# A gated scan with a two-layer expert: the scheduler charges for same-engine results, and the weight range checks move behind the last move of x

## The chip, the cores and the metric

The kernel runs on one core of one Trainium2 chip. The metric is the device time of one execution in microseconds (us), the median of three timed runs.

## What is computed

Two stages follow each other. The first is a gated linear attention with a complex decay per channel, 4 batches by 8 heads by 768 positions with 48 channels a head. Its output, read as 3072 tokens of 384 values, goes through two matrix products with a clipped square between them. Cut to what matters:

```python
mag = np.sqrt(a_re * a_re + a_im * a_im)
scale = np.minimum(mag, 0.999) / (mag + 1e-06)
a_re_n, a_im_n = (a_re * scale, a_im * scale)
for t in range(S):
    new_re = ar * S_re - ai * S_im          # ar, ai: column t of a_re_n, a_im_n
    new_im = ar * S_im + ai * S_re
    S_re, S_im = (new_re + kv, new_im)      # kv: outer product of k[t] and v[t]
    y[:, :, t] = np.einsum('bhd,bhde->bhe', q[:, :, t], S_re)
h = x @ w_in                                # x: y as (3072, 384); w_in (384, 2048)
g = np.where(pos, h, np.where(neg, 0.0, (h + beta) ** 2 / (4.0 * beta)))
return g @ w_out                            # w_out (2048, 384)
```

## The kernel before, in words

The 3072 tokens are cut into 12 units of 256 positions, three units to a batch. Each unit is handled by `gates` and then `attend`. `gates(u)` turns the decay into prefix sums of its logarithm and of its angle (scans on DVE, logarithms, exponentials and sines on ACT), and multiplies k and q with the results. The two large products at its end (L664, in `turn`) give a cosine part, written into the tile x, and a sine part, written into kq. `spread` then moves these, in five DMAs each, into the tiles hd, which have one head side by side with its partner (L674 and on). A unit has two chunks of 128 positions. `attend(u)` forms the scores of a chunk (sc, L816), masks them (am, L824, on DVE), transposes the keys (tp, L760, copied to kT by ACT), multiplies keys with values (dp, L789), adds that to a running state st, and adds the state's and the mask's share into yp (L855, L863). ACT copies yp into xr, and a rest of it into ys.

Two units make a block, so there are six blocks, 0 to 5. When the last yp of a block is copied, six small DMAs (xr<-ys, L367) move the rest into xr. That is the hand-over of x. `split` then writes x as a rounded part xH (ACT, L948) and a remainder xL (DVE, L955), and `moe(blk)` runs 16 steps f. A step has nine matmuls into h (L978: three parts j by the products of xH and xL with the two parts of the weight), an ACT relu into s (L1003, block 0 has two more ACT instructions), DVE's maximum and product into g (L1022 and L1030), ACT's rounded copy gh (L1036) and DVE's remainder gl (L1040), and, three steps later, nine matmuls into the output sums o (L1053). h has two buffers. After the last step ACT copies o to ob (L1080), and three DMAs write it out. While PE works on one block, the other engines prepare the units of the next one, and PE takes their scores and values in between.

The weights come in as 16 packed loads of 768 KB. `weights` unpacks each with three DVE instructions (L395, L404, L413), an ACT copy for the rounded part (L419), and either one DVE subtraction (L424) or four PE matmuls with two ACT copies (L433, L434, L448) for the remainder. The first `LO_PE` of them take the PE way. `ranges(k)` loads each of the 16 packed weights a second time into a tile chk (L380, called at L453 and on) and takes two sums over it on ACT (L461 and L469) to learn whether all weights lie in the range for which the fast path is exact. The results wsum are read once, after the last matmul. chk shares four slots "g" with the tiles ai, x and kq of the units, in a fixed turn.

The order of the work is not written by hand. Each instruction is recorded in a `Plan` with its engine, a cost in ns, what it reads and writes, and, for some, a due time. `Plan.order` runs a list schedule over them: at each point it takes, on the engine that can start soonest, the ready instruction with the earliest due time. An instruction is ready when all that it depends on have ended, plus a delay `LAT` if the earlier one ran on another engine. `emit` writes the instructions in the order of their planned starts, and the engines run that order. Instructions with no due time that comes from a matmul, as the checks, are taken last. Between two PE instructions with a planned gap, `warm` puts matmuls that nobody reads (idle, L1102) until the first one of `moe` has been issued.

Where the table of constants at the top is spoken of: `SLACK` stretches the due times, `EARLY` is the share of block 0 in which the attention of block 1 is due, `HOLD` decides whether an engine leaves a ready instruction for one that is due sooner but not yet ready, and `ABS_ACT` is the number of units whose absolute value runs on ACT and not on DVE.

Of the kernel before, what the change touches and what calls it, by code (L numbers as in the profile page):

```python
# [18 lines left out]
P = 128  # L19
# [15 lines left out]
NBLK = len(BLOCKS)  # L35
# [14 lines left out]


LAT = {"PE": 260, "DVE": 190, "ACT": 190, "SP": 0, "POOL": 200}
DMA_FIX, DMA_END, DMA_ISSUE, LANES = 2400, 50, 470, 8
LOAD, MOVE = 410.0, 240.0
TABLE = 1294
FIRST = 63000
SLACK = 0.96
LAG = 3
SPREADS = 0
SPREAD = ("SP", "ACT")  # L60
HOLD = {'DVE': (0.3, 20000.0), 'ACT': (0.3, 20000.0)}
WINDOW = (0.0, 0.7)
EARLY = (0.0, 0.6)
HEAD = ((15000, 8000), (8000, 2000))
HOME = 4
SPARE = 1
LEAD = 9000
WARM = 0.75
ABS_ACT = 3
LO_PE = 5  # L70
INFLATE = 1.6
SPLIT_DUE = 3000

# [38 lines left out]
class Plan:  # L112
# [3 lines left out]
    def __init__(self):  # L116
        self.ops = []
        self.slots = {}
        self.glued = {}

    def tile(self, slot, make):
        t = Tile_(make, self.slots.get(slot))
# [32 lines left out]
    def order(self):  # L155
        ops = self.ops
# [7 lines left out]
        for i in range(n - 1, -1, -1):  # L164
            eng, cost, _, _, d, dma = ops[i]
# [26 lines left out]
        while done < n:  # L192
            if forced:
                i = forced.pop()
                e = ops[i][0]
                t = max(free[e], ready[i])
            else:
                best = None
                for e in free:
                    while avail[e] and avail[e][0][1] in taken:  # L200
                        heapq.heappop(avail[e])
                    while wait[e] and wait[e][0][1] in taken:
                        heapq.heappop(wait[e])
                    if avail[e]:
                        t = free[e]
                    elif wait[e]:
                        t = max(free[e], wait[e][0][0])
                    else:
                        continue
                    if best is None or t < best[0]:  # L210
                        best = (t, e)
                t, e = best
                while wait[e] and wait[e][0][0] <= t:
                    _, i = heapq.heappop(wait[e])
                    if i not in taken:
                        heapq.heappush(avail[e], (due[i], i))
                d, i = heapq.heappop(avail[e])
                if e in HOLD:
                    late = t + ops[i][1]
                    soon = [  # L220
                        (r, j)
                        for r, j in wait[e]
                        if j not in taken
                        and r < late
                        and due[j] + HOLD[e][1] < d
                        and late - r > HOLD[e][0] * (r - t)
                    ]
                    if soon:
                        heapq.heappush(avail[e], (d, i))
                        free[e] = min(soon)[0]  # L230
                        continue
            taken.add(i)
            eng, cost, _, _, _, dma = ops[i]
            start[i] = t
            free[e] = t + cost
            if dma:
                q = queue.setdefault(eng, [0.0] * LANES)
                t = max(t, q[-LANES])
                q.append(max(t + DMA_FIX, q[-1]) + dma)
                end[i] = q[-1] + DMA_END  # L240
                start[i] = t
                free[eng] = t + cost
            else:
                end[i] = t + cost
            done += 1
            for s in succ[i]:
                left[s] -= 1
                lat = 0 if (ops[s][0] == eng or dma) else LAT[eng]
                ready[s] = max(ready[s], end[i] + lat)
                if not left[s]:  # L250
                    enable(s)
            nxt = self.glued.get(i)
            if nxt is not None and not left[nxt]:
                forced.append(nxt)
# [46 lines left out]
def gated_scan_moe(  # L301
# [32 lines left out]
    pl = Plan()  # L334
# [44 lines left out]
    def load(k, raw):  # L379
        nc.sync.dma_start(raw.rearrange("p n t -> p (n t)"), wl[k].bitcast(U32))  # L380
# [72 lines left out]
    def ranges(k):  # L453
        RAW = tl(turn_of("g", 4), [P, 2 * DM, 2], U32, f"chk_{k}")
        top, low = (lambda: RAW.get()[:, :, 1]), (lambda: RAW.get()[:, :, 0])
        N = 2 * DM
        pl.op("SP", DMA_ISSUE, lambda: load(k, RAW.get()), w=[RAW], dma=P * N * 8 / LOAD)
        pl.op(
            "ACT",
            act(N, acc=True) + 50,  # L460
            lambda: A_.activation(  # L461
                low().bitcast(F32), top().bitcast(F32), AF.Abs, accum_out=wsum[:, 0, k : k + 1]
            ),
            w=[RAW],
        )
        pl.op(
            "ACT",
            act(N, ptr=True, acc=True) + 50,
            lambda: A_.activation(  # L469
                low().bitcast(F32),  # L470
                low().bitcast(F32),
                AF.Relu,
                bias=c_tin,
                scale=-1.0,
                accum_out=wsum[:, 1, k : k + 1],
            ),
            w=[RAW],
        )
# [5 lines left out]
    def gates(u):  # L484
# [3 lines left out]
        N = NJ * U  # L488
# [32 lines left out]
            )  # L521

        def ve(cost, fn, r, w):
            pl.op("DVE", cost, fn, r=r, w=w)

        ac(A, A, AF.Relu, [a], [a], accum_out=acc(0))
        if u > 1:
# [29 lines left out]
        )  # L557
        for j in range(NJ):
            prev = state[:, 0, j : j + 1] if part else 0.0
            ve(  # L560
                100 + U / 0.48,
                lambda j=j, prev=prev: V_.tensor_tensor_scan(  # L562
                    X0()[:, j],
                    X0()[:, j],
                    c_top.to_broadcast([P, U]),
                    prev,
                    op0=ALU.add,
                    op1=ALU.min,
                ),
                [STATE[0]] if part else [],  # L570
                [x0],
            )
        dst = fdec[:, b] if last else state[:, 0]
        ve(80, lambda: V_.tensor_copy(dst, X0()[:, :, U - 1]), [x0], [STATE[0]])
        ac(X1, X0, AF.Exp, [x0], [x1], True, scale=-1.0)
# [8 lines left out]
        ac(I, I, AF.Arctan, [], [i], True)  # L584
        for j in range(NJ):
            prev = state[:, 1, j : j + 1] if part else 0.0
            ve(
                100 + U / 0.48,
                lambda j=j, prev=prev: V_.tensor_tensor_scan(  # L589
                    A()[:, j],  # L590
# [6 lines left out]
                [i] + ([STATE[1]] if part else []),  # L597
                [a],
            )
        c = 1.0 / (2 * math.pi)  # L600
        ve(
            dve(N, True),
# [115 lines left out]

    carry = {}
    xs = {}  # L720

    def attend(u):
        b, part = divmod(u, NPART)
# [114 lines left out]
        def values(c, ams, st):  # L838
# [32 lines left out]
            def tail():  # L871
# [14 lines left out]
                if ub == nb - 1 and c == NC - 1:  # L886
                    for e in range(2):
                        for j in range(NJ):
                            p = 80 * e + 16 * j
                            dma(  # L890
                                16 * T * 4,
                                lambda j=j, e=e: XR.get()[64 * e + D : 64 * e + 64, j],
                                lambda p=p: REST.get()[p : p + 16],
                                r=[REST] + [(XR, q * CH) for q in range(T // CH)],
                                w=[(XR, (e, j))],
                            )

            r = [*ams, V, *hd] + ([st] if st else [])
            return [((16 if st else 8) * 110 + 400, run, r, YP, tail)]
# [63 lines left out]
    def moe(blk):  # L963
# [110 lines left out]
                gemm2(k - LAG)  # L1074
        for m in range(NJ):
            OB = tl(turn_of("s", 3), [P, T], F32, f"ob_{blk}_{m}")
            pl.op(
                "ACT",
                act(T, psum=True),
                lambda m=m, OB=OB: A_.copy(OB.get(), PO[m].get()),  # L1080
# [1 line left out]
                w=[OB],  # L1082
                due=t0 + STEP * (NF + LAG + 1.5),
            )
            dma(
                P * T * 4,
                lambda m=m: out[BLOCKS[blk][0] : BLOCKS[blk][-1] + 1, m].rearrange("n p t -> p n t"),
# [297 lines left out]
```

## Time and profile before

| what | us |
|---|---|
| median of three timed runs | 597.65 |
| lowest and highest of them | 594.56, 598.12 |
| the profiled execution's own time | 595.56 |
| its span in the profile | 593.8 |
| PE busy in the span | 563.2 (95%) |
| DVE busy | 448.7 (76%) |
| ACT busy | 390.3 (66%) |
| mean granted PE clock | 0.982 of full |

The span runs from the first to the last instruction of the profiled execution. Its own time is 1.76 us longer, for what lies around the span. The busy shares are means over a start in which PE waits for its first input, a long middle in which PE is the engine that never rests, and an end in which DVE and ACT have little to do.

### The profile page before, as it was taken

The page shows a single profiled execution, that of the slowest core. Times are in us where ns is not written, and L with a number is a line of the kernel's source. Part 1 is how long each engine was busy: PE and PEld are TensorE (multiplying, and loading weights), DVE is VectorE, ACT ScalarE, POOL GpSimd, SP SyncE. Part 2 cuts the span into 40 slices and gives each one's busy share as a digit, 9 for nine tenths or more (in the row PEclk, how much of TensorE's full clock was granted, in tenths as well). Part 3 has the DMA queues.
Part 4 walks back from the last instruction along what each step waited for, and adds up shares of the span by engine and source line. Part 5 has one row for each costly group of instructions (what it writes and reads, how often), then busy time and mean ns, then how long its engine had stood idle before and what let it go on. Part 6 is the DMA issues. An engine that isn't in the chain of part 4 may idle for free.

```text
span 593.8 us, 9849 instructions
## 1 busy us (share of the span) xinstructions
PE 563.2 (95%) x3874; PEld 475.9 (80%) x3874; DVE 448.7 (76%) x637; ACT 390.3 (66%) x632; POOL 1.5 (0%) x18
## 2 busy tenths in 40 slices
PE   6978988999899999999999999999999999799994
PEld 5767887888788888888888888888888887588883
DVE  3998899999989898897887977977954543555452
ACT  7757779998986767666657586556567475543332
POOL 0000000000000000000000000000000000000000
PEclk9887999999999999999999999999999999999998
DMA  8468363653540610532502512503576744010001
GB/s 350 181 194 233 114 218 110 204 223 108 180 160 19 172 70 0 160 147 67 173 2 81 174 54 81 159 2 95 187 237 167 232 146 175 14 55 0 1 0 59
DMA packets 21798, 74.25 MB, mean 125 GB/s; under 512 B 3888, under 2 KB 8496, under 8 KB 21744
## 3 DMA queue, kind: packets, MB, share of 16 engines
q1 hardware_dynamic: 21744, 73.55, 38.7%
q8 instruction: 32, 0.52, 0.4%
q14 instruction: 22, 0.18, 0.1%
HBM read 48.76 MB, written 4.72 MB: 90 GB/s over the span
## 4 chain that ended last, share of the span: by engine, by line
PE 56%; DVE 18%; DMA 11%; ACT 8%; SPq 3%; issue 2%; DVEq 0%; ACTq 0%
PE o L1053 23%; PE h L978 22%; DMA chk<-in_wl_dram 7%; PE sc L816 4%; SPq L367 3%; PE yp L863 2%; ACT ai L518 2%; PE yp L855 2%; PE dp L789 2%; DVE x L562 2%; ACT chk L469 2%; DVE g L1022 1%; DVE ai L589 1%; ACT x L518 1%; PE tp L760 1%
## 5 line engine op out<-in xcount | busy, mean ns | idle before, releaser
L978 PE MATMUL h<-xH,wi 128*128 128x512 f32 x576 | 180.5, 394 | 6.5 <-DVE g L1022 6.5
L1053 PE MATMUL o<-gh,wo 128*128 128x512 f32 x576 | 179.8, 393 | 0.2 <-ACT gh L1036 0.2
L978 PEld LDWEIGHTS h<-xH,wi 128*128 128x128 f32 x576 | 105.9, 188 | 28.9 <-DVE g L1022 8.2
L1053 PEld LDWEIGHTS o<-gh,wo 128*128 128x128 f32 x576 | 106.4, 188 | 22.3 <-ACT gh L1036 0.8
L1022 DVE TENSOR_TENSOR g<-h,s 128x512 f32<-128x512 f32 x96 | 65.9, 686 | 67.5 <-ACT s L1003 61.5
L1053 PE MATMUL o<-gl,wo 128*128 128x512 f32 x288 | 112.4, 390 | 0.0
L978 PE MATMUL h<-xL,wi 128*128 128x512 f32 x288 | 112.3, 390 | 0.0
L1036 ACT CAST gh<-g 128x512 fp32r<-128x512 f32 x96 | 59.2, 618 | 61.0 <-DVE g L1030 59.9
L1040 DVE TENSOR_TENSOR gl<-g,gh 128x512 fp32r<-128x512 f32 x96 | 66.0, 688 | 36.1 <-ACT gh L1036 35.6
L1003 ACT ACTIVATE s<-h,cst 128x512 f32<-128x512 f32 x96 | 65.7, 685 | 39.5 <-PE h L978 35.0
L518 ACT ACTIVATE ai<-ai 128x768 f32<-128x768 f32 x51 | 42.9, 843 | 33.7 <-DVE ai L609 10.9
L1053 PEld LDWEIGHTS o<-gl,wo 128*128 128x128 f32 x288 | 54.1, 188 | 12.1 <-DVE gl L1040 0.6
L978 PEld LDWEIGHTS h<-xL,wi 128*128 128x128 f32 x288 | 54.1, 188 | 11.6
L1030 DVE SCALAR_TENSOR_TENSOR g<-s,g 128x512 f32<-128x512 f32 x80 | 55.3, 691 | 2.6
L816 PE MATMUL sc<-hd 96*128 96x128 f32 x384 | 49.7, 278 | 0.0
L816 PEld LDWEIGHTS sc<-hd 96*128 96x128 f32 x384 | 46.9, 191 | 2.2
L863 PE MATMUL yp<-am,V 128*64 128x128 f32 x384 | 36.4, 279 | 1.3 <-DVE am L824 1.3
L1102 PEld LDWEIGHTS idle<-mask,ident 128*128 128x128 f32 x226 | 31.6, 221 | 2.6 <-POOL mask masks.py:66 1.7
L1102 PE MATMUL idle<-mask,ident 128*128 128x128 f32 x226 | 32.1, 305 | 1.7 <-POOL mask masks.py:66 1.7
L824 DVE TENSOR_TENSOR am<-sc,mask 128x512 f32<-128x512 f32 x48 | 32.5, 682 | 1.1 <-PE sc L816 0.9
L855 PE MATMUL yp<-hd,st 96*64 96x128 f32 x320 | 32.1, 278 | 1.0 <-DVE am L824 1.0
L461 ACT ACTIVATE chk<-chk 128x768 f32<-128x768 f32 x16 | 14.5, 905 | 21.5 <-DMA chk<-in_wl_dram 21.5
(87 smaller groups left out, 637.6 us busy)
## 6 DMA issues: line engine op xcount, KB each, us to landing
chk<-in_wl_dram SPq DMA_DIRECT2D x16, 768.0 KB, 5.2
kq<-in_kq_dram SPq DMA_DIRECT2D x12, 768.0 KB, 4.8
ai<-in_ari_dram SPq DMA_DIRECT2D x11, 768.0 KB, 6.2
hd<-x SPq DMA_DIRECT2D x24, 288.0 KB, 3.8
hd<-kq SPq DMA_DIRECT2D x24, 288.0 KB, 4.6
raw_i<-in_wl_dram SPq DMA_DIRECT2D x8, 768.0 KB, 6.0
raw_o<-in_wl_dram SPq DMA_DIRECT2D x8, 768.0 KB, 4.6
V<-in_v_dram SPq DMA_DIRECT2D x12, 384.0 KB, 3.2
```

Source lines behind the costliest of these rows:

```text
L518: lambda: A_.activation(out(), src(), f, **kw),
L816: PE_.matmul(SC.get()[:, i, :], t[:, 0, cs], t[:, 1, cs], start=True, stop=True)
L855: PE_.matmul(o, st.get().rearrange("p h e -> p (h e)")[:, lo : lo + 64], head(h)[:, 1, cs], start=True, stop=False,)
L863: PE_.matmul(o, V.get()[:, c, lo : lo + 64], ams[g].get()[:, 2 * pr + e, :], start=st is None, stop=True,)
L978: PE_.matmul(H.get(), weight["i", f // 2].get()[:, f % 2, part, sl], x.get()[:, j, :], start=j == 0 and n == 0, stop=j == NJ - 1 and n == 2,)
L1003: lambda: A_.activation(SS.get(), H.get(), AF.Relu, bias=c_half, scale=-0.5 if spare else 0.5),
L1022: lambda: V_.tensor_tensor(G.get(), H.get(), SS.get(), op=ALU.max),
L1030: lambda: V_.scalar_tensor_tensor(G.get(), SS.get(), 1.0, G.get(), op0=ALU.min, op1=ALU.mult),
L1036: pl.op("ACT", act(T), lambda: A_.copy(GH.get(), G.get()), r=[G], w=[GH])
L1040: lambda: V_.tensor_tensor(GL.get(), G.get(), GH.get().bitcast(F32), op=ALU.subtract),
L1053: PE_.matmul(PO[m].get(), weight["o", f // 2].get()[:, f % 2, part, sl], g.get(), start=f == 0 and n == 0, stop=f == NF - 1 and n == 2,)
L1102: PE_.matmul(idle["h1"], ident, mask, start=True, stop=True)
```

## The change

`Plan.order` now charges a delay `SAME` (122 ns on DVE, 128 on ACT) where an instruction reads or overwrites what an earlier one on its own engine left. Only the second and third scan of a unit, which work on other columns than the scan ahead of them, are exempt (the set `loose`). The constants are set anew. And the second load of each weight, with the checks that read it, may start only when the six moves of x of the last block and all output copies of the blocks ahead of it are done.

```diff
 LAT = {"PE": 260, "DVE": 190, "ACT": 190, "SP": 0, "POOL": 200}
+SAME = {"PE": 0, "DVE": 122, "ACT": 128, "SP": 0, "POOL": 0}
-SLACK = 0.96
+SLACK = 1.0
-HOLD = {'DVE': (0.3, 20000.0), 'ACT': (0.3, 20000.0)}
+HOLD = {'DVE': (2, 0.0), 'ACT': (2, 0.0)}
-EARLY = (0.0, 0.6)
+EARLY = (0.15, 0.7)
-ABS_ACT = 3
-LO_PE = 5
+ABS_ACT = 4
+LO_PE = 3
...
-                lat = 0 if (ops[s][0] == eng or dma) else LAT[eng]
+                lat = LAT[eng]
+                if dma or s in self.loose:
+                    lat = 0
+                elif ops[s][0] == eng:
+                    lat = SAME[eng]
...
-        pl.op("SP", DMA_ISSUE, lambda: load(k, RAW.get()), w=[RAW], dma=P * N * 8 / LOAD)
+        pl.op(
+            "SP",
+            DMA_ISSUE,
+            lambda: load(k, RAW.get()),
+            w=[RAW],
+            dma=P * N * 8 / LOAD,
+            after=[*handover[NBLK - 1], *finals],
+        )
...
+            if j:
+                pl.loose.add(i_)
...
+                            handover.setdefault(blk, []).append(i)
...
+            if blk < NBLK - 1:
+                finals.append(i)
```

In the rows of the order the lines of the changed kernel are higher by some 6 to 21 than those of the kernel before (L367 is L373, L380 is L386, L664 is L681, L978 is L997). A number behind a name tells buffers apart and is new in each program.

SP issues the DMAs. At the end of block 4 it has, before, the last loads of chk, then the six moves of x of block 5 and the three output DMAs of block 4:

```order
L380 DMA chk_4607<-in_wl_dram 128x1536
L380 DMA chk_4614<-in_wl_dram 128x1536
L380 DMA chk_4675<-in_wl_dram 128x1536
L380 DMA chk_4681<-in_wl_dram 128x1536
L367 DMA xr_4184<-ys_4186 16x512 x6
L367 DMA out_dram<-ob_0_4849 128x2x256
```

In the changed kernel SP has at that place:

```order
L373 DMA V_4376<-in_v_dram 128x768
L373 DMA xr_4187<-ys_4189 16x512 x6
L373 DMA out_dram<-ob_0_4796 128x2x256
L373 DMA out_dram<-ob_1_4809 128x2x256
L373 DMA out_dram<-ob_2_4827 128x2x256
L386 DMA chk_4838<-in_wl_dram 128x1536
L386 DMA chk_4840<-in_wl_dram 128x1536
```

All 16 loads of chk have moved behind the moves of x and the outputs. On ACT, where 29 of the 32 checks stood among the steps of block 4 and three ahead of them, all 32 now stand between s of step 2 and s of step 13 of block 5.

PE, ahead of the first matmul of block 0's `moe`, has before the first chunk of unit 2 (the end of it: dp, then the first half of the next chunk's scores):

```order
L789 MATMUL dp_0_786<-V_569,kT_83 64x48 x8
L789 MATMUL dp_0_786<-V_569,kT_84 64x48 x8
L816 MATMUL sc_0_1_806<-hd_0_601 128x128
L816 MATMUL sc_0_1_806<-hd_1_603 128x128
L816 MATMUL sc_0_1_806<-hd_0_601 128x128
L816 MATMUL sc_0_1_806<-hd_1_603 128x128
L978 MATMUL h_0_816<-xH_782,wi_142 128x512 x2
```

In the changed kernel the last dp of unit 1 is followed by idle matmuls, and unit 2 comes after the first h:

```order
L807 MATMUL dp_1_664<-V_116,kT_83 64x48 x8
L807 MATMUL dp_1_664<-V_116,kT_84 64x48 x8
L1123 MATMUL idle<-mask,ident 128x128 x26
L997 MATMUL h_0_752<-xH_714,wi_142 128x512 x2
L997 MATMUL h_0_752<-xL_722,wi_142 128x512
L997 MATMUL h_0_752<-xH_714,wi_142 128x512 x2
L997 MATMUL h_0_752<-xL_722,wi_142 128x512
L997 MATMUL h_0_752<-xH_714,wi_142 128x512 x2
L997 MATMUL h_0_752<-xL_722,wi_142 128x512
L834 MATMUL sc_0_0_771<-hd_0_658 128x128
```

The whole first chunk of unit 2, with half of the second chunk's scores, has moved from ahead of the first matmul of `moe` to behind it.

DVE, in the start, has before the two last products of unit 1 (x_123, then kq_112) with four other instructions between them:

```order
L664 TENSOR_TENSOR x_123<-kq_112,ai_98 128x1536
L395 TENSOR_SCALAR y_o_343<-raw_o_190 128x768
L404 SCALAR_TENSOR_TENSOR raw_o_190<-raw_o_190,y_o_343 128x768
L531 TENSOR_TENSOR ai_277<-ai_277 128x768
L534 TENSOR_SCALAR ai_277<-ai_277 128x768
L664 TENSOR_TENSOR kq_112<-kq_112,ai_98 128x1536
L824 TENSOR_TENSOR am_0_0_391<-sc_0_0_366,mask 128x512
```

In the changed kernel:

```order
L681 TENSOR_TENSOR x_123<-kq_109,ai_98 128x1536
L681 TENSOR_TENSOR kq_109<-kq_109,ai_98 128x1536
L401 TENSOR_SCALAR y_i_358<-raw_i_120 128x768
L544 TENSOR_TENSOR ai_274<-ai_274 128x768
L547 TENSOR_SCALAR ai_274<-ai_274 128x768
L842 TENSOR_TENSOR am_0_0_377<-sc_0_0_363,mask 128x512
```

The two products of unit 1 now follow each other, ahead of unit 2's first instruction (L531, now L544), which waits for ACT.

## Rows read from the trace of the kernel before

**Rows 1.** Windows: start:end, length, each engine's busy us (instructions), PEclk, DMA share, GB/s.
```profile
0.00:87.64 87.64, 73.07 (x689) 64.68 (x689) 73.30 (x95) 64.08 (x98) 1.48 (x18) 0.90 0.66 212
87.64:165.00 77.36, 74.31 (x470) 61.92 (x469) 75.83 (x107) 71.00 (x111) 0.00 (x0) 1.00 0.51 170
165.00:440.00 275.00, 275.00 (x1953) 233.69 (x1952) 228.36 (x323) 183.08 (x292) 0.00 (x0) 1.00 0.33 105
440.00:515.00 75.00, 69.81 (x457) 57.45 (x456) 34.22 (x52) 46.94 (x94) 0.00 (x0) 1.00 0.51 160
515.00:593.80 78.80, 71.06 (x314) 58.12 (x312) 36.95 (x63) 25.24 (x40) 0.00 (x0) 0.98 0.07 22
```

**Rows 2.** Timeline, end of block 4: start, length, instruction, [idle before <-releaser].
```profile
505.07 0.91 ACT L461 ACTIVATE chk<-chk 128x768 f32<-128x768 f32 x1 [1.27 <-DMA chk<-in_wl_dram]
...
509.32 0.73 PE L978 MATMUL h<-xH,wi 128*128 128x512 f32 x2 [2.76 <-DVE g L1022]
```

**Rows 3.** Waits, whole span, ACT's for chk: us in total, times, longest.
```profile
ACT chk L461 <- DMA chk<-in_wl_dram: 21.5, 13, 4.0
```

**Rows 4.** Timeline of ACT in block 4, checks and an s.
```profile
473.96 0.91 ACT L461 ACTIVATE chk<-chk 128x768 f32<-128x768 f32 x1 [0.31 <-DMA chk<-in_wl_dram]
...
474.86 1.00 ACT L469 ACTIVATE chk<-chk,cst 128x768 f32<-128x768 f32 x1
...
476.80 0.68 ACT L1003 ACTIVATE s<-h,cst 128x512 f32<-128x512 f32 x1
477.38 1.01 ACT L469 ACTIVATE chk<-chk,cst 128x768 f32<-128x768 f32 x1
```

**Rows 5.** DMA view, 463 to 506 us in 40 slices.
```profile
GB/s 214 248 260 377 326 326 389 354 160 34 0 0 29 206 389 257 286 244 69 0 8 0 0 160 366 314 251 280 91 0 0 0 91 337 383 387 200 69 11 61
```

**Rows 6.** Timeline of ACT and DVE in one step of block 5, and the next s.
```profile
575.84 0.69 ACT L1003 ACTIVATE s<-h,cst 128x512 f32<-128x512 f32 x1 [1.29 <-PE h L978]
...
576.56 0.69 DVE L1022 TENSOR_TENSOR g<-h,s 128x512 f32<-128x512 f32 x1 [1.28 <-ACT s L1003]
...
579.92 0.69 ACT L1003 ACTIVATE s<-h,cst 128x512 f32<-128x512 f32 x1 [1.29 <-PE h L978]
```

**Rows 7.** Timeline of the hand-over of block 0 (PE, SP's queue and ACT).
```profile
76.70 0.44 PE L855 MATMUL yp<-hd,st 96*64 96x128 f32 x4 [0.54 <-DVE am L824]
...
79.53 2.05 PE L816 MATMUL sc<-hd 96*128 96x128 f32 x16
80.55 4.08 SPq L367 DMA_DIRECT2D xr<-ys  x6
82.82 0.64 PE L1102 MATMUL idle<-mask,ident 128*128 128x128 f32 x4
...
86.16 1.66 ACT L948 CAST xH<-xr 128x512 fp32r<-128x512 f32 x3 [2.43 <-DMA xr<-ys]
87.64 0.71 PE L978 MATMUL h<-xH,wi 128*128 128x512 f32 x2
```

**Rows 8.** Windows, as rows 1, of unit 2's chunk ahead of block 0.
```profile
79.53:87.64 8.11, 7.15 (x105) 6.72 (x101) 7.86 (x12) 5.68 (x11) 0.00 (x0) 1.00 0.60 192
```

**Rows 9.** Timeline of DVE in the start.
```profile
43.45 1.75 DVE L664 TENSOR_TENSOR x<-kq,ai 128x1536 f32<-128x1536 f32 x1
...
48.60 0.96 DVE L531 TENSOR_TENSOR ai<-ai 128x768 f32<-128x768 f32 x1 [1.86 <-ACT ai L518]
49.59 0.56 DVE L534 TENSOR_SCALAR ai<-ai 128x768 f32<-128x768 f32 x1
50.07 1.75 DVE L664 TENSOR_TENSOR kq<-kq,ai 128x1536 f32<-128x1536 f32 x1
...
75.97 0.68 DVE L824 TENSOR_TENSOR am<-sc,mask 128x512 f32<-128x512 f32 x1
```

**Rows 10.** Timeline: a PE gap in the start.
```profile
39.64 0.58 PE L433 MATMUL rest_o<-raw_o,ident 128*128 128x384 f32 x1 [2.77 <-ACT ai L518]
```

**Rows 11.** Windows, as rows 1, behind that gap.
```profile
40.00:47.00 7.00, 6.30 (x23) 5.13 (x22) 6.60 (x7) 2.85 (x6) 0.00 (x0) 0.53 0.86 230
```

More of the change, by code (lines that the diff above doesn't have):

```diff
@@ L119, in __init__ @@
         self.glued = {}
+        self.loose = set()
     def tile(self, slot, make):
@@ L523, in ve @@
         def ve(cost, fn, r, w):
-            pl.op("DVE", cost, fn, r=r, w=w)
+            return pl.op("DVE", cost, fn, r=r, w=w)
         ac(A, A, AF.Relu, [a], [a], accum_out=acc(0))
@@ L559, in gates @@
             prev = state[:, 0, j : j + 1] if part else 0.0
-            ve(
+            i_ = ve(
                 100 + U / 0.48,
@@ L586, in gates @@
             prev = state[:, 1, j : j + 1] if part else 0.0
-            ve(
+            i_ = ve(
                 100 + U / 0.48,
@@ L599, in gates @@
             )
+            if j:
+                pl.loose.add(i_)
         c = 1.0 / (2 * math.pi)
@@ L720, in gated_scan_moe @@
     xs = {}
+    handover, finals = {}, []
     def attend(u):
@@ L889, in tail @@
                             p = 80 * e + 16 * j
-                            dma(
+                            i = dma(
                                 16 * T * 4,
@@ L1076, in moe @@
             OB = tl(turn_of("s", 3), [P, T], F32, f"ob_{blk}_{m}")
-            pl.op(
+            i = pl.op(
                 "ACT",
```

## The prediction

> **What bounds the kernel now.** I read the busy time by stage first (windows that cut the span where `moe` starts, where block 1 starts, and around block 4), then PE's and ACT's waits, the timelines of the places that these name, the DMA view, and last the order of both kernels. PE is the bound, but not everywhere in the same way [rows 1]. From 165 to 440 us it is busy for 275.00 of 275.00 us: nothing done on DVE or ACT there can pay. Up to 87.64, where the first matmul of `moe` runs, PE counts 73.07 us busy, but part of that is filler, and what it waits for is the chain through DVE and ACT that makes the first two units. From 87.64 to 165 three engines are full at once: DVE 75.83 of 77.36 us, PE 74.31, ACT 71.00; PE's idle time is 3.05. From 440 to 515, where the checks of the weights stand, PE idles 75.00 - 69.81 = 5.19 us although ACT has only 46.94 us of work. From 515 on PE runs without rivals and then leaves the copies and the output to the end; I expect nothing of that tail to change.
>
> The 5.19 us have a visible cause. At 505.07 ACT begins a check that it waited 1.27 us for, on a load of chk; at 509.32 PE begins an h after an idle 2.76 us, released by DVE's g [rows 2], which needs ACT's relu s. ACT runs in order, so an s that stands behind a check is late by that check's wait. In the whole span ACT waits 21.5 us for chk, in 13 waits, the longest 4.0 [rows 3]. The DMA rate between 463 and 506 us has stretches of zero between peaks of 389 GB/s [rows 5]: the loads don't come too slowly, they start too late, since a slot "g" must come free first.
>
> **The change part by part.** Everything is counted against the profiled execution (own time 595.56, span 593.8 us).
>
> *The checks leave block 4.* The PE idle time of that stretch goes: -5.2 us. If some of it belongs to other hand-overs, less goes, so the bounds are -5.2 and -3. The nearest evidence for the full amount is the 275 us ahead of it, in which the same kind of work without checks costs no idle time [rows 1].
>
> *The checks enter block 5.* All 32 now stand on ACT between s of step 2 and s of step 13. A check's two passes take .90 (473.96 to 474.86) and .97 (two of them and an s fill 474.86 to 477.38: 2.52 - .58, halved), an s .58 [rows 4]. A step of block 5 lasts 579.92 - 575.84 = 4.08 us [rows 6]. In 11 steps, 44.9 us, ACT has 16 x 1.87 = 29.9 us of checks and 22 instructions (s and gh) x .58 = 12.8, so 42.7: it fits, with 2.2 us over. It also has slack: h has two buffers and its matmuls take half a step, so s and g of a step (.69 and .69, with the hand-over some 1.5 us) may be 2 x 4.08 - 2.04 - 1.5 = 4.6 us late before PE feels it. Together ACT can wait about 2.2 + 4.6 = 6.8 us for chk in this block at no cost. And the reason for waits is smaller: no unit is left that takes the slots "g", so chk has all four. At the peak of [rows 5] a load of 786 kB takes 2.0 us, while ACT needs 44.9 / 16 = 2.8 per check. What is queued behind a waiting check is s, then g, h, o. I take +0.5; the bounds are 0 and +14.7, the latter if ACT waits the 21.5 us of [rows 3] again, less 6.8. I stay near the lower one because the load has a third of its time to spare.
>
> *The start.* The sine product of unit 1 stood behind a DVE instruction that waited 1.86 us for ACT, at 50.07; it can now begin at 43.45 + 1.75 = 45.20, 4.9 us sooner [rows 9]. Down the order of DVE, the am ahead of the last yp of block 0 (75.97) comes some 4.7 us sooner, and that yp, 76.70 before [rows 7], at about 72.0. Against it, SP now issues five moves of hd ahead of the six of xr, all on one queue; the six take 4.08 us, .68 each [rows 7]. Five at that pace are 3.4 us, of which I take 1.3 to lie behind the last copy of yp (before, 3.85 us passed between that yp and the first xr, time enough for the rest). So xr runs from 77.1 to 81.2, xH starts 1.5 us later as before (84.63 to 86.16), and the first h 1.48 us after that: 84.2 in place of 87.64. That is -3.4; the bounds are -4.7 (no hold) and 0 (the moves of hd wait for data of their own).
>
> *Unit 2's chunk moves behind that h.* Before, PE filled the hand-over with it: 7.15 us busy, of which .64 were filler [rows 7, 8]. These 6.5 us now come after the first h, in a stretch where PE has no room to spare: +6.5. In their old place stand 26 idle matmuls that nobody needs. So the earlier hand-over buys PE a hole, not time, unless block 0's own idle time shrinks.
>
> *Block 0's idle time* (3.05 us): kept. DVE is at 98% there [rows 1]; between the splits of blocks 0 and 1 the order counts 107 DVE rows for 104, at 75.83 / 107 = .71 us each 2.1 us more. Bounds -3.05 and +4. I take 0, as two effects (a longer PE stretch, more work on DVE) pull against each other.
>
> *LO_PE and ABS_ACT.* Two weights' remainders move from PE and ACT to DVE (two subtractions of about .96, by the length of the product at 48.60 [rows 9]), one absolute value (.56, as the short one at 49.59) from DVE to ACT. DVE gains some 1.3 us; the 4.7 above holds that already. SLACK, HOLD and EARLY only reorder.
>
> *SAME.* The delay costs no time itself; it spreads dependent neighbours. On DVE their number falls from 172 to 154. In [rows 9] a dependent instruction starts .99 us after one of .96, an independent one .48 after one of .56: .03 late against .08 early, so .11 us each, and 18 x .11 = 2.0 us of DVE over the whole span, mostly where PE waits for nothing. 0, with bounds -2.0 and 0.
> On this the Trainium skill speaks against the change: "VectorE: DVE Perf Modes", section "The DRAIN you can't avoid", has it that the next operation starts only when the pipe has emptied, and that a semaphore between two operations costs nothing extra. By that the 2.0 us would be 0. The rows show the .11 us, and the measurement decides; the sum is the same by either.
>
> The sum: -5.2 + 0.5 - 3.4 + 6.5 + 0 + 0 = -1.6. Own time 594.0. The median of the runs, 597.65, lies .35% above the profiled execution; on that scale it is 596.1. I give 595.0, between the two.
>
> **The rivals.** *Faster.* Units are ready sooner in block 0, since PE's stretch there is longer than DVE's: DVE ends by 84.2 + 77.4 + 2.1 = 163.7, PE by 165 - 3.4 + 6.5 = 168.1, so the 3.05 us of idle time may close; and SP may not hold xr (-1.3). -1.6 - 4.35 = -6.0, so about 590.6 on the scale of the forecast. For it: PE would then have 4 us more slack than DVE. Against: ACT, at 92%, has more to do there.
>
> *The clock.* PE ends the last dp of unit 1 near 74.8 and the first h would start at 84.2: a hole of 9.4 us, in which the 26 idle rows (52 matmuls) last 6.7 to 8.3 us (.128 each as the scores at 79.53, or .16 as the idle ones at 82.82 [rows 7]). 1 to 3 us stay open. An idle time of 2.77 us, ended at 39.64 [rows 10], was followed by a granted clock of .53 from 40 to 47 [rows 11]; one of 2.76 at 509.32 was not (1.00 in the window to 515) [rows 1, 2]. If it falls for about 5 us, PE does half as much: +2.5, own time 596.5, still no measurable change.
> The Trainium skill, "TensorE: Matmul & The Clock Gate", section "HAM oscillation — how this bites in real kernels", tells of kernels in which waits for DMA between batches of matmuls put the array back to the low clock, so that the next batch starts cold. The hole ahead of block 0 is of this kind, a wait for xr.
>
> *Late checks (slower).* The load of a weight can start only when ACT has ended both passes of the check that holds its slot, and s, due at once, is taken ahead of checks. If ACT waits as long as in [rows 3], PE gets 14.7 us of idle time in place of the .5: -1.6 + 14.2 = +12.6, some 609. The change loses from 8.9 us of waiting on (6.8 + 1.6 + .5), .56 per check, and by over 1% (6.0 us) from 14.9 on. For it: 13 of the 16 checks waited before. Against: they shared the slots with units then, and had stretches of zero rate.
>
> *New waits in the long middle.* A new order of units may put a late DVE or ACT result ahead of PE in the 275 us that had none. Four waits like that at 509.32 give -1.6 + 11.2 = +9.6, some 606. For it: the order there is new throughout. Against: DVE is busy 83% there and ACT 67% [rows 1].
>
> *The delay does nothing.* If the planned 122 ns don't show in the run, the sum stays: 594.0.
>
> **How the numbers follow.** Forecast .47, the clock .11, the delay without effect .04: these are within 1% of before (which is about what a measurement of this kernel can tell from no change), together .62. Faster case .22. Late checks .10 and new waits .06, together .16. The forecast alone spans 592 to 598. The range goes down past the faster case to 588.5, and up to 603, short of the late checks: about .06 left out below and .13 above.
>
> **What would show it.** Right: the first h near 84 us, with unit 2's first scores behind it; PE busy for 75 of the 75 us from 440 to 515; ACT's waits for chk all in block 5 and below 6.8 us in sum; the idle time of block 0 still near 3 us; the last matmul only 1 to 2 us sooner. Wrong: an h of block 5 with an idle time ended by g while ACT waits for chk; a granted clock near .5 behind the hole at 84 us; idle time of PE between 165 and 440; block 1 starting before 165.

## The result, and the profile after

The changed kernel takes 591.34 us, the median of ten runs (587.51 to 592.48); the kernel before, run beside it, 597.26 (593.97 to 598.30). The ratio is 0.9907, with a 95% interval of 0.9882 to 0.9932: faster by 0.9%, more than its own noise, and at the edge of the 1% that the prediction called "the same". The forecast of 595.0 was 3.7 us too high; the range of 588.5 to 603 holds the result. The profiled execution has a span of 589.0 us against 593.8, so 4.8 us less; its own time is 590.78.

The stages of the changed kernel, cut where its first matmul of `moe` runs (columns as in [rows 1]):

```profile
0.00:84.13 84.13, 68.75 (x639) 62.32 (x639) 69.19 (x89) 58.92 (x89) 1.49 (x18) 0.92 0.60 198
84.13:165.00 80.87, 79.85 (x552) 66.95 (x553) 78.11 (x109) 72.30 (x113) 0.00 (x0) 0.98 0.55 179
165.00:440.00 275.00, 275.00 (x1950) 233.64 (x1949) 228.33 (x327) 180.77 (x285) 0.00 (x0) 1.00 0.31 97
440.00:515.00 75.00, 75.00 (x490) 63.30 (x489) 37.81 (x57) 24.99 (x44) 0.00 (x0) 1.00 0.11 30
515.00:589.00 74.00, 66.68 (x296) 54.88 (x294) 34.52 (x59) 51.77 (x101) 0.00 (x0) 0.96 0.54 193
```

Against [rows 1]: from 440 to 515 us PE is now busy for 75.00 of 75.00 us, where it idled 5.19. ACT's work there has halved (24.99 for 46.94) and stands in the last stretch (51.77 for 25.24), where PE's idle time is 7.32 us, all of it behind the last matmul, against 7.74. Block 0's stretch has 1.02 us of idle time where it had 3.05. The first h has come 3.51 us sooner.

ACT's waits for chk, in the list of waits of the changed kernel, which answers to [rows 3]:

```profile
ACT chk L474 <- DMA chk<-in_wl_dram: 4.6, 4, 2.5
```

4.6 us in sum, less than the 6.8 that block 5 was said to bear, and PE felt none of it. Now the hand-over of block 0, first PE's timeline, then SP's queue and ACT (compare [rows 7]):

```profile
73.98 0.44 PE L873 MATMUL yp<-hd,st 96*64 96x128 f32 x4
...
76.81 6.07 PE L1123 MATMUL idle<-mask,ident 128*128 128x128 f32 x52
84.13 0.73 PE L997 MATMUL h<-xH,wi 128*128 128x512 f32 x2 [1.25 <-ACT xH L967]
85.42 0.80 PE L997 MATMUL h<-xL,wi 128*128 128x512 f32 x1 [0.56 <-DVE xL L974]
86.01 1.05 PE L997 MATMUL h<-xH,wi 128*128 128x512 f32 x2
...
88.57 2.03 PE L834 MATMUL sc<-hd 96*128 96x128 f32 x16
```

```profile
75.26 2.54 SPq L373 DMA_DIRECT2D hd<-x  x4
77.89 0.53 SPq L373 DMA_DIRECT2D hd<-kq  x1
78.53 4.51 SPq L373 DMA_DIRECT2D xr<-ys  x6
...
83.47 1.64 ACT L967 CAST xH<-xr 128x512 fp32r<-128x512 f32 x3
```

The five moves of hd do stand ahead of xr on SP, and the first h is at 84.13 (84.2 was forecast). Behind the 52 idle matmuls, PE stood open for 1.25 us and once more for .56, and then an xH pair took 1.05 us where it takes .61: the clock fell for some 3 us (85.4 to 88.6).

An account of the 4.8 us, by this execution against that of before. Up to the first h it is 3.51 us ahead. From there the stretches from one block's first h to the next block's compare like with like. Blocks 0, 1 and 4, before and then in the changed kernel:

```profile
87.64:167.60 79.96, 76.91 (x490) 64.36 (x488) 78.39 (x111) 73.54 (x115) 0.00 (x0) 1.00 0.52 174
167.60:253.67 86.07, 86.07 (x603) 72.94 (x602) 75.22 (x109) 60.25 (x95) 0.00 (x0) 1.00 0.31 94
425.40:518.45 93.05, 87.86 (x595) 72.41 (x594) 45.90 (x66) 58.76 (x117) 0.00 (x0) 1.00 0.51 160
```

```profile
84.13:168.41 84.28, 83.26 (x567) 69.75 (x567) 81.49 (x114) 75.67 (x117) 0.00 (x0) 0.98 0.56 180
168.41:256.16 87.75, 87.75 (x617) 74.72 (x616) 74.75 (x109) 60.09 (x94) 0.00 (x0) 1.00 0.33 104
427.89:514.08 86.19, 86.19 (x594) 72.83 (x593) 47.32 (x67) 31.13 (x55) 0.00 (x0) 1.00 0.13 35
```

Blocks 2, 3 and 5 agree within .01 us. Block 4 is 6.86 us shorter: 5.19 us of idle time, and 1.67 us in which PE counted as busy, most of it in matmuls that took longer next to the waits. Blocks 0 and 1 are 4.32 and 1.68 us longer, 6.00 in sum. In it are the idle time of block 0, 1.02 for 3.05, -2.03; the clock, +1.4 (from the first h to the sc behind it 88.57 - 84.13 = 4.44 us, and 3.01 in the run with more filler below); and unit 2's chunk, what is left, +6.6. Behind the last matmul, 7.51 for 7.93 us, -.42. The sum is -3.51 - 6.86 + 6.00 - .42 = -4.8.

### The profile page after: what moved, and what is told of

It reads as the page before. It is cut to its first block, busy times and chain, and to the rows that moved or that the text cites. A ratio compares the mean times of both kernels' runs of the same rounds, so it can differ in the third digit from the quotient of the medians.

```text
span 589.0 us, 9922 instructions
## 1 busy us (share of the span) xinstructions
PE 565.3 (96%) x3920; PEld 481.1 (82%) x3920; DVE 448.0 (76%) x638; ACT 388.8 (66%) x629; POOL 1.5 (0%) x18
## 4 chain that ended last, share of the span: by engine, by line
PE 73%; DVE 18%; ACT 4%; DMA 2%; issue 1%; DVEq 0%; ACTq 0%
PE o L1072 29%; PE h L997 29%; PE sc L834 6%; PE yp L873 2%; PE yp L881 2%; PE dp L807 2%; PE tp L778 1%; DVE am L842 1%; DVE x L681 1%; ACT ai L531 1%; DMA raw_o<-in_wl_dram 1%; DVE kq L681 1%; DVE kq L594 1%; DVE raw_i L410 1%; DVE raw_o L410 1%
## 5 line engine op out<-in xcount | busy, mean ns | idle before, releaser
L997 PE MATMUL h<-xH,wi 128*128 128x512 f32 x576 | 181.6, 396 | 1.7 <-ACT xH L967 1.2
L997 PEld LDWEIGHTS h<-xH,wi 128*128 128x128 f32 x576 | 106.3, 189 | 23.1 <-ACT xH L967 1.4
L997 PE MATMUL h<-xL,wi 128*128 128x512 f32 x288 | 113.2, 393 | 0.6 <-DVE xL L974 0.6
L997 PEld LDWEIGHTS h<-xL,wi 128*128 128x128 f32 x288 | 54.4, 189 | 12.7 <-DVE xL L974 1.0
L531 ACT ACTIVATE ai<-ai 128x768 f32<-128x768 f32 x52 | 43.7, 844 | 30.9 <-DVE ai L626 14.0
L834 PEld LDWEIGHTS sc<-hd 96*128 96x128 f32 x384 | 48.1, 195 | 2.6 <-DMA hd<-x 0.3
L1123 PE MATMUL idle<-mask,ident 128*128 128x128 f32 x284 | 37.5, 295 | 1.7 <-POOL mask masks.py:66 1.7
L1123 PEld LDWEIGHTS idle<-mask,ident 128*128 128x128 f32 x284 | 37.1, 211 | 2.5 <-POOL mask masks.py:66 1.7
```

What stands on the lines that cost most here:

```text
L531: lambda: A_.activation(out(), src(), f, **kw),
L834: PE_.matmul(SC.get()[:, i, :], t[:, 0, cs], t[:, 1, cs], start=True, stop=True)
L997: PE_.matmul(H.get(), weight["i", f // 2].get()[:, f % 2, part, sl], x.get()[:, j, :], start=j == 0 and n == 0, stop=j == NJ - 1 and n == 2,)
L1123: PE_.matmul(idle["h1"], ident, mask, start=True, stop=True)
```

## The experiments

Two theories stood at the start. A: the checks carry the gain. B: the new order of the start and of block 0 carries it. The kernels of one group ran on one chip, beside the kernel before; between groups, which are on different chips, ratios compare better than times.

### First group: the checks' move alone, all but the move, and the filler

```diff
 (e1_chk_only: before, plus)
-        pl.op("SP", DMA_ISSUE, lambda: load(k, RAW.get()), w=[RAW], dma=P * N * 8 / LOAD)
+        pl.op("SP", ..., after=[*handover[NBLK - 1], *finals])
 (e2_no_chk_move: changed kernel, minus)
-            after=[*handover[NBLK - 1], *finals],
 (e6_more_filler: changed kernel, in warm(i, n); e7_no_filler has n = 0)
+        if kinds.get(i) == "moe" and "over" not in idle:
+            n += 4
```

> The kernel before with one part of the change: the loads of chk may start only after the last moves of x and the outputs. The order of the other engines' instructions stays as before. Theory A (the checks carry the gain): PE's idle time of 5.2 us between 440 and 515 us goes, none comes in block 5, so the ratio to before is 0.990 to 0.992, as good as the whole change; the first h stays at 87.6 us and block 0 keeps its 3 us of idle time. Rival B (the new order of the start and of block 0 carries it): at best half of it shows, ratio 0.995 or more.

> The changed kernel without that one part: the checks are back among the steps of block 4, all other parts of the change stay. Theory A: PE idles some 5 us again between 440 and 515 us, waits of ACT for chk come to about 20 us, and the ratio to before is 0.998 to 1.003. Rival B: the ratio stays below 0.996.

Measured: e1 592.44 us, ratio 0.9942 (0.9918 to 0.9967); e2 593.97, 0.9972 (0.9941 to 1.0003). Neither theory had it: the move alone gives some 0.6%, not 0.9, and all the rest without it some 0.3%, with an interval from 0.6% down to nothing. In e1's trace PE is indeed busy for 75.00 of the 75 us. What was lost showed at the end, in the timelines of ACT, DVE and PE there:

```profile
583.14 0.99 ACT L482 ACTIVATE chk<-chk,cst 128x768 f32<-128x768 f32 x1
584.25 0.17 DVE L1169 TENSOR_SCALAR wsum<-wsum 128x16 f32<-128x16 f32 x1 [2.47 <-ACT chk L482]
584.79 0.19 PE L1174 MATMUL fp<-ok,cst 128*1 128x4 f32 x2 [2.25 <-DVE ok L1170]
```

The last check runs at 583.14, behind s of step 15; DVE waits 2.47 us for its sum, and the small matmul fp of the flag, the last PE work, 2.25 us for DVE. In the changed kernel the last check is over by 570.4 and fp waits for nothing:

```profile
569.43 0.99 ACT L482 ACTIVATE chk<-chk,cst 128x768 f32<-128x768 f32 x1
...
581.49 0.19 PE L1174 MATMUL fp<-ok,cst 128*1 128x4 f32 x2
```

e2's profile caught its fastest run (591.33 us): ACT waited 16.6 us for chk there, and PE idled only 1.03 us from 440 to 515. Its median is 2.6 us longer. How long PE idles in block 4 in the other runs no trace shows.

> The changed kernel with 30 in place of 26 rows of idle matmuls in the hole ahead of the first h (4 rows are 8 matmuls, about .94 us of the 1.25 that were left open). If the open 1.25 us is what lowers the granted clock behind the hole (0.67 from 84 to 88 us), the clock is 1.00 there, the matmuls from 85.4 to 88.6 us take their usual time, and the last matmul comes 1.5 us sooner: ratio to before 0.988. If the wait for xL, .56 us behind the first h, does it, or the hole as a whole, clock and time stay as in the changed kernel: 0.991.

> The changed kernel with none of the idle matmuls in the hole ahead of the first h, which then is open for 7.3 us. If filler is worth something there, the granted clock from 84 us on is near 0.5 and for longer than the 3 us of the changed kernel; five us at half the clock cost 2.5 where the changed kernel lost 1.5, so a ratio to before of 0.992 to 0.995. If the clock falls behind this hole anyway, the time is that of the changed kernel, 0.991.

Measured: e6 591.02 us, 0.9902 (0.9873 to 0.9930); e7 592.74, 0.9932 (0.9903 to 0.9960). The times of e6 and the changed kernel can't be told apart, but the clock can. Windows of e6, of the changed kernel and of e7, in this order:

```profile
84.00:88.00 4.00, 3.08 (x15) 2.16 (x15) 3.96 (x7) 3.43 (x7) 0.00 (x0) 1.00 0.54 144
```

```profile
84.00:88.00 4.00, 3.31 (x8) 2.40 (x9) 3.97 (x6) 2.75 (x5) 0.00 (x0) 0.67 0.60 159
```

```profile
84.00:88.00 4.00, 2.44 (x5) 1.53 (x6) 3.97 (x7) 4.00 (x6) 0.00 (x0) 0.50 0.53 143
88.00:92.00 4.00, 4.00 (x19) 3.52 (x18) 2.41 (x4) 1.88 (x4) 0.00 (x0) 0.59 0.90 322
```

With .94 us more of filler, and .36 us left open, the granted clock stays at 2.4 GHz, though the wait of .56 us for xL is still there; without filler it is at 1.2 GHz from 82 to 88 us. The mean granted clock of the single runs agrees: .983 to .988 in e6, .981 to .987 in the changed kernel, .970 to .980 in e7. So the wait for xL alone doesn't make the fall, and filler in the hole prevents or shortens it here (the last section shows that the open length by itself doesn't decide). In time, e7 is 1.7 us behind e6 on the same chip, and eight of its twelve runs lie above the slowest of e6's. What the last 8 of the 60 idle matmuls bring doesn't show in the time: in e6's trace it is 496.1 us from the first h to fp, the last matmul, for 497.4 in the changed kernel, but the first h came 1.0 us later behind unit 2's load (39.5 us for 38.5; more of this load in the last section).

### Second group: where the last check stands, the loads, SAME, EARLY

```diff
 (e8_chk_placed: e1, plus, in Plan.order)
-                if e in HOLD:
+                if e in HOLD and d < 1e11:
 (e5_no_chk_load: before, in ranges)
-        pl.op("SP", DMA_ISSUE, lambda: load(k, RAW.get()), ...)
+        pl.op("SP", DMA_ISSUE, lambda: RAW.get(), ...)
-                low().bitcast(F32), top().bitcast(F32), AF.Abs, ...
+                wide(low().bitcast(F32)), held().bitcast(F32), AF.Abs, ...
 (e3_no_same: changed kernel)
-SAME = {"PE": 0, "DVE": 122, "ACT": 128, "SP": 0, "POOL": 0}
+SAME = {"PE": 0, "DVE": 0, "ACT": 0, "SP": 0, "POOL": 0}
 (e9_early_old: changed kernel)
-EARLY = (0.15, 0.7)
+EARLY = (0.0, 0.6)
```

> The run with the checks' move alone, but ACT no longer leaves a check aside for an s that is due soon: the last check stands ahead of s of step 13, as in the changed kernel, and not behind s of step 15. Nothing else moves. Theory A2 (the late last check keeps a part of the gain): in the run with the move alone, the final matmul waited 2.25 us for the flag that reads the last check; without this wait the ratio to before falls from 0.994 to 0.990 or 0.991. Rival: the tail wait is an accident of one execution, or the reads of the weights cost elsewhere in block 5; the ratio stays at 0.994.

Measured: 588.97 us, 0.9847 (0.9801 to 0.9893). The interval lies wholly below e1's. ACT's last check, and fp on PE:

```profile
565.05 0.97 ACT L482 ACTIVATE chk<-chk,cst 128x768 f32<-128x768 f32 x1
...
578.74 0.19 PE L1174 MATMUL fp<-ok,cst 128*1 128x4 f32 x2
```

The wait at the end is gone, and by the traces the places of the checks on ACT in block 5 are all that differs from e1's order. It was `HOLD` as before, by which ACT leaves a check aside for an s, that had pushed the last check behind s of step 15. The medians, of two chips, differ by 3.5 us, more than the 2.25. From block 5's first h to fp e1 takes 70.7 us and e8 67.4, as the changed kernel does, so the late checks cost 3.3 us there and not the one wait alone; the first h in e8's profile is also 2.5 us sooner than in e1's (86.10, 88.60), of which the last section says more. The ratio is below the 0.990 or 0.991 that were expected. Unforeseen: e8 is faster than the whole change.

> The kernel before, its checks where they are in block 4, but without the 16 loads into chk: the checks read the unpacked weights, which lie in memory already. ACT's work and its order stay, so does the turn of the slots; the sums of the second part are those of other numbers. If ACT's waits for the loads make PE's idle time in block 4, PE idles less than 1 us between 440 and 515 us, and the ratio to before is 0.990 to 0.992. If the checks' own 30 us of work, or the slots, make it, 3 us and more of the idle time stay, with a ratio of 0.995 and more.

Its time, 14.6 ms, says nothing: by the other numbers the weights seem out of range, and the slow exact path runs behind the fast one. The fast part is in the trace:

```profile
440.00:515.00 75.00, 75.00 (x486) 63.19 (x485) 37.74 (x56) 50.19 (x99) 0.00 (x0) 1.00 0.12 30
```

All of ACT's work is still there (50.19 us), and PE doesn't idle; block 4 takes 86.19 us from first h to first h, as in the changed kernel. So it was ACT's waits for the loads that made the 5.19 us, not its work on the checks. (The traffic of the loads is gone too, 30 GB/s for 160, and a slot is given back sooner where nothing is loaded into it; neither is told apart.) Why the loads came late is in the waits of SP's queue, before and in the changed kernel (us in total, times, longest):

```profile
SPq L380 <- ACT chk L469: 32.5, 11, 6.4
SPq L386 <- ACT chk L482: 29.0, 12, 5.4
```

A load waits for ACT's second pass over an earlier chk: it is the checks that hold up each other's slots (a product of a unit did so once, for 1.3 us, before), and they do so in block 5 too, where PE doesn't feel it. The moves of x of block 5, which stood behind the loads in this queue, were not held by them: before, they start at 503.82, as soon as ACT's last copy into ys (503.52, .27 us long) has ended.

> The changed kernel with the delay for results on the same engine set to nothing, all else as changed. Predicted: dependent neighbours on DVE come back to about the number before, DVE is busy up to 2 us longer, none of it on the path: the ratio to before stays 0.990 to 0.992. Rival: the delay is worth more than its 2 us, since it sets what is taken first at the hand-over and in block 0; then the ratio is 0.994 or more.

Measured: 594.04 us, 0.9918 (0.9889 to 0.9946), as predicted no difference that shows against 0.9907, though the interval just reaches the rival's 0.994. DVE is busy for 447.8 us in its trace and 448.0 in the changed kernel's: the up to 2 us more didn't come.

> The changed kernel with EARLY at (0.0, 0.6) as before: the first scores of unit 2 (2 us of PE) come back into the hole ahead of the first h, behind 24 rows of idle matmuls. If what moves behind the first h is paid in full there (the prediction's +6.5 us for a whole chunk), this gives back 2 us, and the hole is closed for the clock too, 1.5 us: ratio to before 0.985 to 0.988. If DVE paces block 0 and PE has room there, the 2 us don't show in the time: 0.990.

Measured: 596.58 us, 0.9968 (0.9939 to 0.9998), slower than either side of the expectation. The scores that came back into the hole were not free to run:

```profile
89.51 0.46 PE L834 MATMUL sc<-hd 96*128 96x128 f32 x2 [1.69 <-DMA hd<-kq]
...
89.73 0.71 PE L997 MATMUL h<-xH,wi 128*128 128x512 f32 x2
```

They wait 1.69 us for unit 2's own moves, the yp ahead of them is at 77.81 and not at 73.98, and the first h comes at 89.73.

### Third group: the rules and the sizes, beside the changed kernel

```diff
 (e10_after: the changed kernel; e11_chk_placed_again: e8; e12_new_rules_old_sizes: changed kernel with)
-ABS_ACT = 4
-LO_PE = 3
+ABS_ACT = 3
+LO_PE = 5
 (e13_old_rules_new_sizes: e8 with ABS_ACT = 4, LO_PE = 3)
```

> The changed kernel itself, beside the next three on one chip. By the traces so far (the first h 38.5 us after ACT gets the load of unit 2, 497.4 us from there to the last matmul): ratio to before 0.989 to 0.992. It is the measure for the other three.

> The checks' move alone with the last check ahead of s of step 13, a second time, beside the changed kernel. Theory A2 (the start with unit 2's chunk in the hole is the better one; what the rest of the change brings is only that the last check doesn't come late): its trace had the first h 40.7 us after ACT gets the load of unit 2 and 492.6 us from there to the last matmul, 2.6 us less than the changed kernel in sum, so 0.4% faster than the changed kernel: 0.985 to 0.987. Rival: its first result came from a chip whose runs of before were long, and it is level with the changed kernel, 0.990.

Measured: the changed kernel 591.66 us, 0.9913 (0.9881 to 0.9944); e11 589.43, 0.9867 (0.9826 to 0.9908). Four of e11's six runs (587.46 to 590.79) lie below the fastest of the changed kernel's eight (590.07 to 593.31). The intervals against before overlap by a quarter of a per cent, so the 2.2 us between the medians, though e8 in the second group points the same way, are likely and not beyond doubt. The traces say where they come from. PE's timeline around the first h of e8, whose hand-over is that of e11:

```profile
82.35 0.44 PE L873 MATMUL yp<-hd,st 96*64 96x128 f32 x4 [0.44 <-DVE am L842]
...
86.10 0.72 PE L997 MATMUL h<-xH,wi 128*128 128x512 f32 x2
...
93.62 0.73 PE L997 MATMUL h<-xH,wi 128*128 128x512 f32 x2 [1.99 <-DVE g L1041]
```

The chunk of unit 2 fills the hole, as before, and the first h follows it at 86.10 with no wait; the wait of 1.99 us behind it is part of block 0's idle time. From there to fp e8 and e11 take 492.6 and 493.4 us, the changed kernel in its two profiles 497.4 and 497.3: 4.3 us more on the mean, for a first h that is 2.2 us sooner when counted from the moment that ACT gets the load of unit 2 (38.5 us for 40.7). That leaves 2.1 us, what the medians show.

> The changed kernel with ABS_ACT at 3 and LO_PE at 5 as before. Unit 2's chunk stays behind the first h, and two weights' remainders go back to PE and ACT. If the sizes are worth the 1.3 us that they were costed at on DVE, and DVE sets the start, this is 1 to 2 us faster than the changed kernel, 0.988; if PE's filler time and ACT hide them, level with it.

> The checks' move alone, last check ahead of s of step 13, with ABS_ACT at 4 and LO_PE at 3 as in the changed kernel. The order keeps unit 2's chunk ahead of the first h. Theory A2: it is as fast as the run without the new sizes, within 1.5 us (0.985 to 0.988), and faster than the changed kernel, since the rules, not the sizes, put the chunk behind the first h. Rival: the sizes are the useful part of the rest, and it is 2 us or more faster than the run without them, 0.982 or less.

Measured: e12 592.92 us, 0.9940 (0.9916 to 0.9965); e13 593.39, 0.9937 (0.9909 to 0.9966). Neither is as expected: e12 is not faster than the changed kernel (eleven of its twelve runs lie above seven of e10's eight), and e13 lies outside both of its ranges. The new sizes cost about 4 us under the old rules (e13 against e11) and perhaps bring 1 under the new (e10 against e12, intervals overlap). In e13's trace the first h comes 43.0 us after the load of unit 2, 2.4 later than in e11, with scores that wait .86 us for hd, and that load itself was 1.1 us later there; from the first h on it takes 492.7 us, like e8. So in this pair the sizes act in the start alone, 1.1 us of it perhaps by the chance of the load, and how they do depends on the order around them. Which instruction of the start makes it was not tried.

## Why the prediction was right or wrong

**The checks leave block 4: right in its cause, too small in its size.** The idle time of 5.19 us went, and e5 shows the cause as named, ACT's waits for the loads. But the block became 6.86 us shorter for the -5.2 forecast, outside the bounds: the step counted idle time alone and left out the slower matmuls around each wait. That chk would have all four slots didn't end the waits for them, as SP's queue shows. **The checks enter block 5: right for the changed kernel,** 0 for the +.5; ACT waited 4.6 us and PE none. But the step named s, g, h and o as all that stands behind a late check. It left out the flag: the sums wsum end in fp, ahead of the end of the kernel. With "I expect nothing of that tail to change" the prediction passed over the one way in which late checks did cost time (3.3 us in e1, 2.25 of them in the wait of fp). The changed kernel escapes it because its order ends the checks before s of step 13, which the order showed and the text even quoted, without seeing what for.

**The start: right in its sum, by two errors that cancel.** -3.4 forecast, -3.51 measured. Inside, the yp came 2.7 us sooner and not 4.7. The sine product did move up, but the instruction it passed did not: unit 2's first one on DVE starts at 48.71, as at 48.60 before [rows 9], with a longer wait.

```profile
45.67 0.84 ACT L531 ACTIVATE ai<-ai 128x768 f32<-128x768 f32 x1 [3.33 <-DMA ai<-in_ari_dram]
...
48.71 0.96 DVE L544 TENSOR_TENSOR ai<-ai 128x768 f32<-128x768 f32 x1 [3.38 <-ACT ai L531]
```

Behind it stands ACT, and behind ACT the load of unit 2. By counting rows down the order, the prediction moved work past a wait that a DMA ends. The other way, from the last yp to the first h took 10.15 us where 12.2 was forecast, above all since xH starts .43 us behind xr, and the h .66 us behind that, where 1.5 had been taken for each.

**Unit 2's chunk: right.** +6.5 forecast, +6.6 left for it in the account by blocks; 4.9 us of it are paid in block 0 and 1.7 in block 1, in which 16 more matmuls of scores stand.

**Block 0's idle time: the step that failed most.** "Kept", 3.05 us, and it fell to 1.02. Before, it was two waits for DVE's g. The changed kernel has the second one only, beside the .56 us for xL that were shown above:

```profile
94.36 0.73 PE L978 MATMUL h<-xH,wi 128*128 128x512 f32 x2 [1.49 <-DVE g L1022]
...
161.00 0.73 PE L978 MATMUL h<-xH,wi 128*128 128x512 f32 x2 [1.56 <-DVE g L1022]
```

```profile
163.50 0.72 PE L997 MATMUL h<-xH,wi 128*128 128x512 f32 x2 [0.46 <-DVE g L1041]
```

The first is filled by unit 2's chunk. In e1, e8 and e11, where the chunk stands ahead of the first h, it is there (2.00, 1.99 and 1.95 us); in both profiles of the changed kernel, in e2, e6 and e7, where the chunk stands behind it, it isn't. So the prediction charged the chunk in full and left out that a part of it runs while PE would wait. The rival that spoke of it had the reason, a PE stretch longer than DVE's. The second wait is smaller in e1 too (.44), whose order up to there is that of before; why is open.

**The clock rival came true beside it,** at .67 from 84 to 88 us and +1.4 us in some 3 us, where 2.5 had been priced for 5. **SAME: right,** nothing that can be measured (e3). **Late checks and new waits in the long middle** did not come: 275.00 of 275.00 us.

So the forecast of -1.6 became -4.8: the idle time of block 0 (-2.0), the checks leaving block 4 (-1.7) and entering block 5 (-.5), the tail (-.4) and the start (-.1) on one side, the clock (+1.4) and the chunk (+.1) on the other. Of the signs that were named, the idle time of block 0 near 3 us and a last matmul only 1 to 2 us sooner (it was 4.4) did not come, and one of the signs of being wrong did, a clock near .5 behind the hole. Another, block 1 starting before 165, could not tell: its first h is at 167.60 before, so 165 was not the start of block 1. The chances put 1% as the mark between same and faster, and the result fell just short of it; at 591.34 us it is .7 us from the faster rival's 590.6 and 3.7 from the forecast. That the sum of so many misses still lies near the forecast is partly luck.

What the checks' move is worth by itself is told by e8 and e11: with the last check kept off the end, 1.5 and 1.3%. The new order of the start and block 0 gives back about 2 us of that (e10 beside e11): the chunk behind the first h costs 4.3 us, net of the wait that it fills, and the first h is only 2.1 us sooner for it. The clock is not the difference, since in their profiles it falls in e8 and e11 too, behind the wait of 2 us in block 0 (.57 from 94 to 98 us in both). Seen from e1 the other parts look like a gain of .3%, but that gain is the end of the last check. e8 is the fastest version of these runs.

## To carry to other kernels

Work that nobody waits for has a reader after all: before moving it late, follow its result to the end of the kernel and count the distance from its last instruction to that reader. The idle time that a profile counts can be less than what the waits cost: compare the lengths of like stretches (here 6.86 us for 5.19). A hand-over that comes sooner is worth no more than what PE does in the hole it leaves: a chunk of real work there did better than filler where it was ready (e11 beside e10), and worse where it had to wait for its own data (e9). And a count of instructions down an engine's order holds only as far as the next wait that a DMA ends.

## What was not expected of the hardware

Kernels with the same instructions in the start got unit 2's load at different times: ACT begins on it at 47.40 (e1), 45.41 (e8) and 45.93 us (e11), and over all the profiles between 44.41 and 47.40. The first h follows it after 40.7 to 41.2 us in these three and after 38.5 to 38.6 in the changed kernel's two and e2, but after 39.5 and 39.9 in e6 and e7, which differ from the changed kernel in the filler alone. So a part of the spread between runs (591.06 to 594.12 us in e1) is likely this load, one profile each being all that there is to show it.

The length of an open hole alone did not tell whether the clock would fall. 1.25 and .56 us behind 52 idle matmuls were followed by .50 from 86 to 88 us (the changed kernel; its second profile and e2 alike), 1.65 and .36 behind 50 by 1.00 from 82 to 92 us (e3, below). Nor did the work ahead of the hole: the wait of 1.95 to 2.00 us in block 0 was followed by a fall in e1, e8 and e11, and by 1.00 from 94 to 102 us in e5, which has the same order of instructions there.

```profile
77.91 5.85 PE L1123 MATMUL idle<-mask,ident 128*128 128x128 f32 x50
85.41 0.73 PE L997 MATMUL h<-xH,wi 128*128 128x512 f32 x2 [1.65 <-ACT xH L967]
86.50 0.50 PE L997 MATMUL h<-xL,wi 128*128 128x512 f32 x1 [0.36 <-DVE xL L974]
```
